# Attention and gated MLP on one core: the scores of the fourth pair of heads from split operands instead of float32 ones

## The chip, the cores and the metric

The kernel runs on one core of one Trainium2 chip. The metric is device microseconds of one execution, lower is better. The kernel before takes 799.14 us in the median of three runs (799.07 to 799.27). The core has five engines that each work through their own instructions in order: PE (matrix products), DVE, ACT and POOL (elementwise work) and SP, which here only issues transfers. Work that depends on another engine's work waits on semaphores; a transfer is waited for in the same way.

## The reference

Eight batches, eight heads, 576 positions, 64 numbers to a head. Attention with a decay, then a gated MLP in which positions are mixed by a matrix:

```python
def _attn_ref(q, k, v, f):
    scores = scale * np.matmul(q, k.transpose(0, 1, 3, 2))
    cum = np.cumsum(np.log(np.clip(f, 0.0001, 1.0)), axis=-1)
    decay = cum[:, :, :, None] - cum[:, :, None, :]
    scores = np.where(causal, -1000000000.0, scores + decay)
    attn = np.exp(scores - np.max(scores, axis=-1, keepdims=True))
    attn = attn / (np.sum(attn, axis=-1, keepdims=True) + 1e-09)
    return np.matmul(attn, v)

def _moe_ref(x, w_in, w_spatial, b_spatial, w_out):
    h = np.maximum(x @ w_in, 0.0)                     # [b, 576, 1024]
    u, v = (h[..., :512], h[..., 512:])
    v_n = (v - mean(v)) / np.sqrt(var(v) + 1e-06)
    v_s = np.einsum('ts,bsd->btd', w_spatial, v_n) + b_spatial[None, :, None]
    return (u * v_s) @ w_out
```

## The kernel before, in words

**Pairs.** The 64 heads are worked on as 32 pairs, P = 0 to 31; four pairs make a batch, so P = 0 to 3 is the whole attention of the first batch. Heads of a pair are h = 0 and 1. Queries and keys of one head lie in one operand of 1216 columns, 640 of queries and 576 of keys, with the 64 dimensions of the head in the partitions. Rows below them carry the decay, so that one product gives score and decay together. The scores of a head (`scores`) are four tiles `sc` of 128 queries by 128, 256, 384 and 512 keys; the last 64 queries of both heads together are two more tiles of 288 keys with one product from each head (`scores_tail`, the "tail"). The first four head tiles are masked and reduced by DVE (L345), exponentiated by ACT (L347) and scaled by POOL (L355) in the buffer `tt` of that head (`tt_67` for h = 0, `tt_68` for h = 1), turned by PE (L401, L414) into `tp`, copied to `ef` (for the first NF = 5 pairs) or split to `eh` and `el`, and multiplied with the values (`attend`, tiles `x`).

**Two ways to make the scores.** Pairs below NQ take their operand as float32: one tile `tf` per head, straight from memory (L288) with two decay rows copied below (L294). One float32 product is two instructions on PE in the trace. From P = NQ on the operand is split in two parts, `hi` and `lo`, whose sum it is: `split(P)` loads the pair's `raw` operand of 128 partitions (L275), ACT rounds it to `hi` (L278) and POOL subtracts to get `lo` in two instructions (L280). `prep(P, h)` then builds two stacked operands per head with six transfers on SP: `ta` holds hi over lo for the queries (L300, L301) and hi again for the keys (L302), `tb` holds hi of the queries (L303), lo of the keys (L304) and four decay rows from `rows_d` (L305). The score is then the sum of two products, one instruction each:

```python
ta = wk.tile([68, QK], F32, name="tf", tag="ta" if P % 2 == 0 else "tb", bufs=2)   # P < NQ
ta = wk.tile([128, QK], F32R, name="ta", tag="ta", bufs=2)                         # P >= NQ
tb = wk.tile([128, QK], F32R, name="tb", tag="tb", bufs=2)
for t in ts:                                                                       # qkt, L260
    mm(o, t[0:r, q0:q0 + 128], t[0:r, k0:k0 + n], first and t is ts[0], final and t is ts[-1])
```

Both ways use the same four buffers: a float32 pair takes two of them (`ta` for even P, `tb` for odd P), a split pair all four. So a split pair's transfers wait for whichever pair had the buffer before.

**Order.** `attention(b)` goes pair by pair: transposes and value products of pair P are written between the scores of pair P + 1. `split(P)` is called in the turn of P - 2, `prep(P, h)` in that of P - 1. `load_first` spreads the loads (L152, L182, L197) and the conversion of the 64-bit weights (`conv64`, L162 to L173, on ACT, DVE and POOL) over the first batch. From then on the MLP of a batch (`moe`) runs between the attention of the next. A scheduler fixes the final order of every engine's instructions when the program is built, from its own estimate of when each can start; on the chip that order doesn't change any more. In the first batch the pool of `sc` tiles has three buffers, and so has that of `tp`.

Of the kernel before, what the change touches and what calls it, by code (L numbers as in the profile page):

```python
# [17 lines left out]

BIG = 1.0e9
NF = 5  # L20
NQ = 4
LEAD = 0.25
S = 576
D = 64
# [14 lines left out]
def attn_gmlp_kernel(ctx: ExitStack, tc: tile.TileContext, qk, v, f, w_in, w_sp, b_sp, w_out, out):  # L39
# [230 lines left out]
    def split(P):  # L270

        if P < NQ:
            return
# [9 lines left out]
    def prep(P, h):  # L283

        p = slice(64 * h, 64 * h + 64)
        if P < NQ:
            ta = wk.tile([68, QK], F32, name="tf", tag="ta" if P % 2 == 0 else "tb", bufs=2)
# [427 lines left out]
```

## Time and profile before

| what | value |
|---|---|
| median of three runs | 799.14 us (799.07 to 799.27) |
| the profiled execution's own time | 797.53 us |
| its span, first to last instruction | 795.7 us |
| mean granted TensorE clock | 0.993 |
| PE busy | 778.9 us, 98% of the span |
| DVE, ACT, POOL busy | 556.6, 534.9, 476.4 us |
| transfers | 103.48 MB, mean 130 GB/s |

In the rows that follow, a row of the timeline gives the start in us from the span's start, the time in us, engine, line, operation, the tiles (out<-in), the shapes and a count; a bracket at its end is the idle time of that engine just before and what ended it. A row of the table by stretch gives for each engine the busy time and the number of instructions in that stretch, then the granted clock of TensorE (1.00 is full speed), the share of time in which the DMA engines were busy, and the rate. PE's instructions overlap: a row's own time is longer than the distance to the next row's start, so what a product costs PE is read from start to start.

### The profile page before, as it was taken

How to read it: one execution, taken by the hardware profiler on the slowest of the kernel's cores; microseconds unless marked ns; L12 is line 12 of the kernel's file. 1: busy time of each engine (PE TensorE's matmuls, PEld its weight loads, DVE VectorE, ACT ScalarE, POOL GpSimd, SP SyncE). 2: the span in 40 equal slices, each digit the busy share in tenths (PEclk: the TensorE clock that was granted, in tenths of full speed). 3: DMA queues.
4: the chain of work that ended last, by engine and by line, in shares of the span. 5: the costliest groups of instructions: out<-in, count | busy, mean ns of one | idle time of the engine just before them, and what ended most of it. 6: DMA issues, size and time to landing. Idle time of an engine off the chain costs nothing.

```text
span 795.7 us, 15502 instructions
## 1 busy us (share of the span) xinstructions
PE 778.9 (98%) x4980; PEld 702.3 (88%) x4981; DVE 556.6 (70%) x1665; ACT 534.9 (67%) x1418; POOL 476.4 (60%) x660
## 2 busy tenths in 40 slices
PE   8999989899999999999999999999999999999997
PEld 4767779798999989998999989999899988998996
DVE  7889778975767667766866668766787658674421
ACT  7787678675777777667766668766686767764431
POOL 5777798664865647465655647554776537643251
PEclk9999999999999999999999999999999999999999
DMA  9967744566454565365454555564555465320001
GB/s 246 239 185 185 188 119 121 119 168 171 103 123 119 153 152 142 102 148 136 104 143 129 133 145 114 131 170 135 141 134 138 108 164 134 78 75 14 28 1 67
DMA packets 41713, 103.48 MB, mean 130 GB/s; under 512 B 6831, under 2 KB 8879, under 8 KB 41568
## 3 DMA queue, kind: packets, MB, share of 16 engines
q1 hardware_dynamic: 41306, 101.96, 49.7%
q8 instruction: 40, 0.66, 0.4%
q10 hardware_dynamic: 326, 0.53, 0.3%
q14 instruction: 41, 0.34, 0.1%
HBM read 39.42 MB, written 10.68 MB: 63 GB/s over the span
## 4 chain that ended last, share of the span: by engine, by line
PE 86%; DVE 6%; ACT 3%; POOL 2%; issue 2%; DMA 1%; ACTq 0%; POOLq 0%; DVEq 0%
PE ps L260 45%; PE sc L260 16%; PE x L260 12%; PE tp L401 8%; PE tp L260 2%; PE tp L414 2%; DVE tt L345 1%; POOL tt L355 1%; DVE el L391 1%; DVE xl L450 1%; DVE wa L163 0%; ACT eh L390 0%; DVE vx L545 0%; ACT tt L347 0%; ACT hi L278 0%
## 5 line engine op out<-in xcount | busy, mean ns | idle before, releaser
L355 POOL TENSOR_SCALAR tt<-tt,sm 128x128 f32<-128x128 f32 (+3 forms) x256 | 142.0, 573 | 74.9 <-DVE sm L351 56.4
L345 DVE CUSTOM_DVE_ANT_0 tt<-sc,zm 128x128 f32<-128x128 f32 (+3 forms) x256 | 122.8, 486 | 85.0 <-PE tp L401 63.4
L390 ACT CAST eh<-tp 128x512 fp32r<-128x512 f32 (+1 forms) x270 | 111.4, 426 | 75.4 <-PE tp L401 50.2
L347 ACT ACTIVATE tt<-tt,nm 128x128 f32<-128x128 f32 (+3 forms) x256 | 144.4, 565 | 23.7 <-DVE nm L345 21.9
L391 DVE TENSOR_TENSOR el<-tp,eh 128x512 fp32r<-128x512 f32 (+1 forms) x270 | 127.2, 485 | 26.2 <-ACT eh L390 23.8
L401 PE MATMUL tp<-ident,tt 128*128 128x128 f32 x640 | 111.6, 277 | 4.1 <-DVE el L391 4.1
L260 PE MATMUL sc<-ta 128*128 128x128 f32 (+1 forms) x336 | 109.1, 330 | 2.5 <-DVE nm L345 2.0
L260 PE MATMUL sc<-tb 68*128 68x128 f32 (+1 forms) x336 | 106.2, 320 | 0.0
L260 PE MATMUL x<-eh,vt 128*128 128x320 f32 (+4 forms) x378 | 102.5, 287 | 0.0
L593 POOL TENSOR_TENSOR gl<-u,gh 128x256 fp32r<-128x256 f32 x64 | 47.7, 745 | 87.7 <-ACT gh L592 78.1
L260 PE MATMUL ps<-xh,win 128*128 128x256 f32 (+1 forms) x464 | 99.3, 304 | 0.4 <-ACT u L570 0.3
L280 POOL TENSOR_TENSOR lo<-raw,hi 128x640 fp32r<-128x640 f32 (+1 forms) x56 | 84.2, 1525 | 16.1 <-ACT hi L278 15.9
L260 PE MATMUL ps<-win,xh 128*128 128x512 f32 x296 | 90.6, 396 | 0.0
L260 PE MATMUL x<-el,vt 128*128 128x256 f32 x324 | 90.1, 303 | 0.0
L401 PEld LDWEIGHTS tp<-ident,tt 128*128 128x128 f32 x640 | 76.3, 141 | 14.2 <-issue 2.7
L449 ACT CAST xh<-x 64x256 fp32r<-64x256 f32 (+1 forms) x128 | 49.8, 394 | 42.3 <-PE x L260 40.3
L260 PEld LDWEIGHTS ps<-xh,win 128*128 128x128 f32 x464 | 76.3, 192 | 2.0 <-ACT u L570 0.9
L260 PE MATMUL ps<-sph,vnh 128*128 128x256 f32 (+1 forms) x240 | 73.2, 305 | 0.4 <-ACT o L618 0.4
L260 PEld LDWEIGHTS x<-eh,vt 128*128 128x128 f32 x378 | 71.3, 190 | 2.5 <-POOL vt L322 0.3
L260 PE MATMUL ps<-wo,gh 128*128 128x512 f32 x224 | 71.9, 405 | 0.0
L260 PEld LDWEIGHTS sc<-ta 128*128 128x128 f32 x336 | 64.3, 191 | 8.6 <-DVE nm L345 4.5
L260 PE MATMUL ps<-sph,vnl 128*128 128x256 f32 (+1 forms) x240 | 71.6, 298 | 0.0
(178 smaller groups left out, 1916.4 us busy)
## 6 DMA issues: line engine op xcount, KB each, us to landing
raw<-in_dram SPq DMA_DIRECT2D x28, 608.0 KB
ta<-hi SPq DMA_DIRECT2D x56, 304.0 KB
vraw<-in_dram SPq DMA_DIRECT2D x32, 320.0 KB
tb<-hi SPq DMA_DIRECT2D x56, 160.0 KB
ta<-lo SPq DMA_DIRECT2D x56, 160.0 KB
out_dram<-o SPq DMA_DIRECT2D x32, 256.0 KB
ta<-hi SPq DMA_DIRECT2D x56, 144.0 KB
tb<-lo SPq DMA_DIRECT2D x56, 144.0 KB
```

The source lines that it names most:

```text
L260: last['mm'] = T.matmul(o, l, r, start=st, stop=sp)
L280: G.tensor_tensor(out=lo[:, c], in0=raw[:, c], in1=f32(hi[:, c]), op=ALU.subtract)
L345: V.tensor_tensor_reduce(out=t, in0=sc[:, 0:n], in1=zm[:, 640 - n:640], scale=-0.125, scalar=3.0e38, op0=ALU.add, op1=ALU.min, accum_out=n ...
L347: last["exp"] = last["exp", P, h, i] = A.activation(t, t, AF.Exp, bias=nm[:, i:i + 1], scale=-1.0, accum_out=se[:, i, 0:1])
L355: G.tensor_scalar(out=t, in0=t, scalar1=sm[:, i:i + 1], scalar2=1.0, op0=ALU.mult, op1=ALU.mult)
L390: A.copy(h_ap, ps)
L391: V.tensor_tensor(out=l_ap, in0=ps, in1=f32(h_ap), op=ALU.subtract)
L401: T.transpose(out=tp[:, (i - c) * 128:(i - c + 1) * 128], in_=tt[h][:, TOFF[i] + 128 * c:TOFF[i] + 128 * c + 128], identity=ident)
L414: T.transpose(out=tp[:, j * 128:(j + 1) * 128], in_=tl[:, c * 128:(c + 1) * 128], identity=ident)
L449: last[P, h] = A.copy(hi, ps[m0:m0 + 64, 0:n])
L450: V.tensor_tensor(out=lo, in0=ps[m0:m0 + 64, 0:n], in1=f32(hi), op=ALU.subtract)
L593: G.tensor_tensor(out=gl[j][:, 0:256], in0=g[:, 0:256], in1=f32(gh[j][:, 0:256]), op=ALU.subtract)
```

## The change

```diff
--- before
+++ after
@@ -18,7 +18,7 @@
 
 BIG = 1.0e9
 NF = 5
-NQ = 4
+NQ = 3
 LEAD = 0.25
 S = 576
 D = 64
```

Pair 3, the fourth and last pair of the first batch, now takes the split way in `split`, `prep` and `qkt`; pairs 0 to 2 stay float32. Its attention weights and values stay float32 (NF is unchanged). Two loads L288 and two copies L294 go; one load L275, one L278, two L280 and twelve transfers L300 to L305 come; 12 float32 products (24 instructions on PE) become 24 products of one instruction.

The scheduler puts much of the first quarter in another order. With buffer numbers left out, PE's first and last rows that differ lie at about 45 and 163 us of the trace; past that, every engine's order is the same as before.

**Pair 3's scores on PE.** Here PE works on the scores of pair 3, head 0 (`sc`), with the transposes of pair 2 (`tp`) and its value products (`x`) between them. Before:

```order
L260 MATMUL sc<-tf 128x256
L260 MATMUL x_601<-ef,vraw 128x192
L260 MATMUL x_601<-ef,vraw 128x64
L401 MATMUL tp<-ident,tt_67 128x128 x2
L260 MATMUL sc<-tf 128x384
L401 MATMUL tp<-ident,tt_67 128x128
L260 MATMUL x_706<-ef,vraw 128x256
L260 MATMUL sc<-tf 128x512
```

The same place with the change:

```order
L260 MATMUL sc<-ta 128x256
L260 MATMUL x_608<-ef,vraw 128x192
L260 MATMUL x_608<-ef,vraw 128x64
L401 MATMUL tp<-ident,tt_67 128x128 x2
L260 MATMUL sc<-ta 128x384
L401 MATMUL tp<-ident,tt_67 128x128
L260 MATMUL sc<-tb 128x128
L260 MATMUL sc<-tb 128x256
L260 MATMUL sc<-tb 128x384
L260 MATMUL x_731<-ef,vraw 128x256
```

The `ta` halves of three tiles stand where the float32 products stood; their `tb` halves come together behind them, and the fourth tile, with the tail, moves behind the first transposes of the next head.

**The transfers for pair 3 on SP.** With the change these rows stand on SP where before there were loads only; a bracket names the semaphores that a row waits on (one of the eight `DMAHW` is that of the transfer eight rows earlier):

```order
L300 DMA ta<-hi 64x1216 [waits DMAHW7_49,PE_49]
L301 DMA ta<-lo 64x640 [waits DMAHW0_49,Pool_49]
L302 DMA ta<-hi 64x576 [waits DMAHW1_49]
L182 DMA w_571<-in_dram 128x4x256 [waits DMAHW2_49]
L182 DMA w_573<-in_dram 128x4x256 [waits DMAHW3_49]
L182 DMA w_575<-in_dram 128x4x256 [waits DMAHW4_49]
L304 DMA tb<-lo 64x576 [waits DMAHW5_49,Pool_49]
L304 DMA tb<-lo 64x576 [waits DMAHW6_49]
```

The last piece of head 0's `tb` (the first of the two L304) is behind three weight loads; L300 waits on PE for the buffer that pair 2's head 0 held.

**Pair 4: the wait of the transfers and the place of the products.** On SP before, the operands of pair 4 were issued in this order (head 0's and head 1's mixed):

```order
L300 DMA ta<-hi 64x1216 [waits DMAHW5_49,Activation_49]
L302 DMA ta<-hi 64x576 [waits DMAHW6_49]
L300 DMA ta<-hi 64x1216 [waits DMAHW7_49]
L303 DMA tb<-hi 64x640 [waits DMAHW0_49,PE_49]
L301 DMA ta<-lo 64x640 [waits DMAHW1_49,Pool_49]
L305 DMA tb<-rows_d 4x1216 [waits DMAHW2_49]
L304 DMA tb<-lo 64x576 [waits DMAHW3_49,Pool_49]
```

With the change:

```order
L305 DMA tb<-rows_d 4x1216 [waits DMAHW6_49,PE_49]
L300 DMA ta<-hi 64x1216 [waits DMAHW7_49,Activation_49]
L302 DMA ta<-hi 64x576 [waits DMAHW0_49]
L303 DMA tb<-hi 64x640 [waits DMAHW1_49]
L301 DMA ta<-lo 64x640 [waits DMAHW2_49,Pool_49]
L300 DMA ta<-hi 64x1216 [waits DMAHW3_49,PE_49]
L304 DMA tb<-lo 64x576 [waits DMAHW4_49,Pool_49]
```

The second L300 fills head 1's `ta`, which pair 3's head 1 now holds until its last score product; before, pair 2 had held it. Head 0's L304 stands right behind that wait.

On PE, the scores of pair 4, head 0, follow the last score product of pair 3, head 1 (the first two rows) like this with the change:

```order
L260 MATMUL sc<-ta 128x512
L260 MATMUL sc<-tb 128x512
L401 MATMUL tp<-ident,tt_67 128x128
L260 MATMUL sc<-ta 128x128
L260 MATMUL sc<-ta 128x256
L401 MATMUL tp<-ident,tt_67 128x128 x2
L260 MATMUL sc<-ta 128x384
L401 MATMUL tp<-ident,tt_67 128x128 x6
L260 MATMUL sc<-tb 128x128
```

Between that last product and the first use of pair 4's `tb` there are nine transposes and three `ta` halves.

## The prediction

> **What bounds the kernel now.** I read the page's busy table first, then the table by stretch around the scores of pair 3, then the chain of waits between 40 and 130 us, since the order changes only there, and last the timeline of PE.
>
> ```profile
> PE 778.9 (98%) x4980; PEld 702.3 (88%) x4981; DVE 556.6 (70%) x1665; ACT 534.9 (67%) x1418; POOL 476.4 (60%) x660
> 40.00:45.00 5.00, 5.00 (x27) 3.56 (x26) 3.60 (x14) 3.94 (x11) 4.29 (x7) 1.00 1.10 356
> 50.00:55.00 5.00, 3.80 (x18) 2.48 (x17) 4.94 (x12) 4.67 (x13) 5.00 (x6) 1.00 0.27 78
> 54.14 1.24 PE L260 MATMUL sc<-tf 66*128 66x288 f32 x4 [1.20 <-DVE nm L345]
> by line: PE x L260 12.8%; PE ps L260 12.6%; PE sc L260 12.3%; POOL tt L355 8.3%; issue 8.2%; PE tp L401 6.6%; DVE tt L345 4.6%; DVE wa L163 4.2%; POOL win L173 2.8%; POOL wa L171 2.8%; POOL vnl L549 2.8%; DVE xl L450 2.1%; DVE spl L205 1.7%
> 81.58 2.14 POOL tt L355 x3
> 83.72 1.27 POOL win L173
> 84.98 1.24 POOL wa L171
> ```
>
> The first row says PE, 98%. Over the whole span that is right: a microsecond of PE work taken away late in the kernel would be a microsecond won. The stretch that the change touches is another matter. At 50 to 55 us PE is busy for 3.80 of 5.00, while DVE (4.94) and POOL (5.00) are full: PE waits 1.20 us for DVE in the middle of pair 3's tail. The chain from 40 to 130 us shows the same: PE's largest lines there are 12.8, 12.6, 12.3 and 6.6%, and from 81.58 us on the chain runs over POOL and DVE pieces, weight conversion among them. So PE time saved at 45 to 60 us is only partly passed on.
>
> **What the scores cost, before and after.** These rows of the timeline are pair 3, head 0, and one half of its tail; below them, the same widths made from split operands in later pairs.
>
> ```profile
> 47.27 0.60 PE L260 MATMUL sc<-tf 66*128 66x256 f32 x2
> 47.71 0.85 PE L260 MATMUL x<-ef,vraw 128*128 128x192 f32 x4
> ...
> 48.77 0.81 PE L260 MATMUL sc<-tf 66*128 66x384 f32 x2
> 49.41 0.27 PE L401 MATMUL tp<-ident,tt 128*128 128x128 f32 x1
> 49.52 0.59 PE L260 MATMUL x<-ef,vraw 128*128 128x256 f32 x2
> 49.96 1.02 PE L260 MATMUL sc<-tf 66*128 66x512 f32 x2
> 50.82 0.49 PE L414 MATMUL tp<-ident,tl 128*128 128x128 f32 x3
> ...
> 51.48 1.24 PE L260 MATMUL sc<-tf 66*128 66x288 f32 x4
> 52.55 0.38 PE L414 MATMUL tp<-ident,tl 128*128 128x128 f32 x2
> ```
>
> ```profile
> 67.30 0.38 PE L260 MATMUL sc<-ta 128*128 128x288 f32 x1
> ...
> 67.94 0.38 PE L414 MATMUL tp<-ident,tl 128*128 128x128 f32 x2
> ...
> 83.02 0.33 PE L260 MATMUL sc<-ta 128*128 128x256 f32 x1
> ...
> 83.31 0.64 PE L260 MATMUL ps<-win,xh 128*128 128x512 f32 x2
> ...
> 85.61 0.42 PE L260 MATMUL sc<-ta 128*128 128x384 f32 x1
> ...
> 86.06 0.40 PE L260 MATMUL sc<-ta 128*128 128x512 f32 x1
> ...
> 86.53 0.49 PE L414 MATMUL tp<-ident,tl 128*128 128x128 f32 x3
> ```
>
> From start to start, float32 takes 0.44 us for 256 keys (47.27 to 47.71), 0.64 for 384, 0.86 for 512 and 1.07 for a tail tile. The two split products take 0.29 (83.02 to 83.31), 0.45, 0.47 and 0.64 (two heads, four products, 67.30 to 67.94). I take the 128-key tile as even. Per head this saves 0.15 + 0.19 + 0.39 = 0.73 us, per tail tile 0.43; twice each makes **-2.3 us of PE work**.
>
> **The work that is added and hidden.** One rounding on ACT and two subtractions on POOL:
>
> ```profile
> 55.29 2.91 POOL L280 TENSOR_TENSOR lo<-raw,hi 128x640 fp32r<-128x640 f32 x2
> 49.19 1.27 POOL L171 TENSOR_TENSOR wa<-w,wa 128x512 f32<-128x512 f32 x1 [4.83 <-DVE sm L350]
> 40.13 0.62 ACT L172 CAST win<-wa 128x512 fp32r<-128x512 f32 x1 [1.13 <-POOL wa L171]
> ```
>
> The 2.91 us on POOL now come at about 37 us, ahead of a wait of 4.83 us for DVE that ends at 49.19; ACT's rounding stands ahead of a wait of 1.13. Both idle times cover them: 0 on the path. Without that cover it would be up to 2.9 us.
>
> What isn't free is DVE. While POOL ran one instruction from 35.98 to 37.25, a DVE instruction that takes 0.41 us elsewhere took 1.41:
>
> ```profile
> 35.98 1.27 POOL L173 TENSOR_TENSOR win<-wa,win 128x512 fp32r<-128x512 f32 x1
> 36.13 1.41 DVE L168 TENSOR_SCALAR wa<-w 128x512 uint32<-128x512 uint32 x1
> ...
> 46.84 0.41 DVE L168 TENSOR_SCALAR wa<-w 128x512 uint32<-128x512 uint32 x1
> ```
>
> Two more POOL instructions can hold up DVE twice by 1.0 us, 2.0 in all; DVE has 1.40 us idle in the stretch from 40 to 45 (5.00 less 3.60). That bounds the cost at 0 to 0.6, if all the idle time serves; I take **+0.3**. [...]
>
> **The wait that goes and the wait that comes.** PE's 1.20 us at 54.14 stand between two products of the tail. With the change the tail comes after the next head's first transposes, so I count that wait as gone: **-1.2** (0 if it only moves). Its place is taken by pair 4. Head 0's last transfer, L304, stands on SP right behind a wait for pair 3's last score product on PE. From that product PE has nine transposes at 0.11 (49.41 to 49.52) and three `ta` halves, some 0.5 by half of the pairs above: 1.5 us of work before it needs that transfer.
>
> ```profile
> 58.23 0.46 SPq L304 DMA_DIRECT2D tb<-lo  x1
> 62.08 0.28 PE L260 MATMUL sc<-tb 68*128 68x128 f32 x1
> ```
>
> From issue to use the same transfer took at most 3.85 us before (58.23 to 62.08; PE didn't wait there, so it may have landed sooner). With one issue of 0.5 ahead of it, it lands up to 4.4 us after the release: a stall of 0 to 2.9 us. I take **+2.4**, near the upper end, since that row is the only one for it. Behind the stalled product stand the value products and all scores of pair 4, and DVE waits for these; behind the blocked L300 on SP stand the rest of pair 4's pieces.
>
> **Pair 3's own last transfer.** L304 follows three weight loads of 512 KB.
>
> ```profile
> 38.29 0.60 PE L401 MATMUL tp<-ident,tt 128*128 128x128 f32 x4
> w<-in_dram SPq DMA_DIRECT2D x12, 512.0 KB
> 54.00:62.00 8.00, 7.86 (x41) 5.89 (x41) 7.03 (x27) 6.61 (x19) 8.00 (x9) 1.00 0.92 209
> ```
>
> `ta` can be issued when pair 2's tail is through, at 38.29 us where the next transposes start; three issues of 0.5 to 0.6 later, at 40, the loads go out. 1.57 MB take 4.4 us at the 356 GB/s of 40 to 45 us, and with 3.85 for the transfer itself it lands at 48.3. PE needs it where the row at 49.52 now stands, less 0.7 for what is no longer ahead of it (0.44 and 0.64, less half of 0.29 and of 0.45): 48.8. I take 0, with 2.6 as the other end, since at the 209 GB/s of 54 to 62 us the loads take 7.5.
>
> **The sum**, against the profiled execution's own 797.53: -2.3 - 1.2 + 2.4 + 0.3 = -0.8, so 796.7. The median of the runs stands 1.6 above that execution; on its scale **798.3**. What 0.8 becomes until 163 us, where both orders are the same again, no row tells: PE waits and gaps of about 2 us at a time lie on that way.
>
> **Rivals.** *The saving goes through, faster.* L304 lands as fast as PE gets there, or POOL's scaling is the later wait in both kernels; then -2.3 - 1.2 = -3.5 is left and 795.6. For it: PE's row at 62.08 didn't wait. Against: DVE is full at 50 to 55 us and gets nothing back.
>
> *The late low parts decide, slower.* One mechanism: L304 comes too late for PE at both pairs. If the loads ahead of it run at 209 GB/s, pair 3 stalls by 2.6; pair 4 by 2.9; and TensorE's clock drops after that.
>
> ```profile
> 108.00:110.00 2.00, 0.88 (x4) 0.48 (x4) 1.90 (x6) 2.00 (x6) 1.10 (x3) 1.00 0.00 0
> 110.00:112.00 2.00, 1.07 (x6) 0.67 (x6) 2.00 (x8) 2.00 (x5) 1.36 (x1) 0.95 0.00 0
> 112.00:114.00 2.00, 2.00 (x10) 2.00 (x9) 2.00 (x5) 2.00 (x6) 2.00 (x2) 0.50 0.00 0
> 114.00:116.00 2.00, 2.00 (x12) 2.00 (x12) 2.00 (x3) 0.63 (x3) 2.00 (x3) 0.69 0.36 71
> ```
>
> PE is busy for 0.88 and 1.07 of two times 2 us, and the granted clock falls right behind that: means of 0.95, 0.50 and 0.69 over 2 us each, so 2 x (0.05 + 0.50 + 0.31) = 1.7 us of full speed are lost. Sum: -2.3 - 1.2 + 2.6 + 2.9 + 1.7 = +3.7, so 802.8. It decides once the stalls and the clock together pass 3.5 + 1.6. Against it: the loads of 40 to 45 us ran at 356. [...]
>
> *The change doesn't do what it says.* If a split product costs PE what a float32 one does, -2.3 falls away: +1.5, 800.6. The rows of both kinds stand against it.
>
> **How the numbers follow.** Forecast 0.42, faster rival 0.28, late low parts 0.25, no saving 0.05. About 0.2% (1.6 us) is what a measurement of this kernel can tell from no change. The forecast's own range is 797.5 to 800.7, all within it. The faster rival and 0.02 from a forecast that gains on its way to 163 us give faster 0.30; the late low parts and 0.03 of the case without a saving give slower 0.28; 0.42 is left for the same. The range, 795.3 to 802.5, takes in the faster rival's 795.6 and most of the way to the slower one's 802.8, which has all three unknown costs (2.6, 2.9 and 1.7) at their far ends; no more than 2 in 10 lie outside.
>
> **What would show it.** Twelve more products `ta` and `tb`, and `tf` down by 24, with the pairs' starts at the distances above. PE's wait at pair 3's tail gone; a wait of PE for a transfer or for POOL at about 60 us, ahead of pair 4's first `tb` product, of 2 to 3 us. No wait of PE at pair 3's first `tb`. POOL's wait ahead of 49 us shorter by about 3. It is wrong if PE waits for pair 3's `tb`, if pair 4's runs on without a wait, or if the places and lengths of the half-clock stretches differ: each of them moves the time by more than my whole sum.

## The result and the profile after

The changed kernel takes 808.69 us (median of four runs, 806.87 to 809.62), the kernel before 799.2 us beside it. The ratio is 1.0115, with a 95% interval from 1.0096 to 1.0133: slower, where I had forecast 798.3 us and no difference that can be told. A second set of four runs of the changed kernel, in a later job, gave 805.8 us (803.56 to 808.16), ratio 1.0087 (1.0061 to 1.0113).

The profiled execution of the changed kernel took 809.62 us, 12.1 us more than the one of the kernel before; its span is 807.8 us. The page's busy row is nearly what it was:

```profile
PE 783.6 (97%) x4981; PEld 707.5 (88%) x4981; DVE 554.8 (69%) x1665; ACT 537.5 (67%) x1419; POOL 479.2 (59%) x662
```

PE is now busy for 783.6 us instead of 778.9, although it has less to do: busy time counts instructions at half clock at their longer time (a `ta` product of 288 columns takes 0.59 us at 56.09, where the clock is halved, and 0.30 at 59.25). So this row can't say where the time is. The timeline of PE can; these are its rows from 45 to 125 us that begin with a wait of 0.44 us or more, and one (70.58) that was expected to:

```profile
52.40 0.64 PE L260 MATMUL sc<-tb 68*128 68x128 f32 x3 [3.54 <-DMA tb<-lo]
...
58.91 0.37 PE L260 MATMUL sc<-ta 128*128 128x288 f32 x1 [1.88 <-DMA ta<-hi]
...
67.46 0.33 PE L401 MATMUL tp<-ident,tt 128*128 128x128 f32 x1 [0.76 <-POOL tt L355]
...
69.22 0.55 PE L401 MATMUL tp<-ident,tt 128*128 128x128 f32 x3 [0.64 <-POOL tt L355]
70.20 0.72 PE L401 MATMUL tp<-ident,tt 128*128 128x128 f32 x3 [0.44 <-POOL tt L355]
70.58 1.10 PE L260 MATMUL sc<-tb 68*128 68x128 f32 x3
...
86.09 2.54 PE L260 MATMUL x<-ef,vraw 128*128 128x320 f32 x10 [1.43 <-DVE xl L450]
...
119.53 0.38 PE L260 MATMUL x<-eh,vt 128*128 128x256 f32 x1 [1.07 <-POOL vt L322]
...
122.24 0.61 PE L260 MATMUL sc<-ta 128*128 128x288 f32 x1 [2.04 <-DVE nm L345]
```

The first two are new: 3.54 us for pair 3's `tb` (head 0), 1.88 us for its `ta` (head 1). The table by stretch shows what stands around them, first before, then after (PE, PEld, DVE, ACT, POOL busy, clock, DMA share, GB/s):

```profile
48.00:52.00 4.00, 4.00 (x20) 2.73 (x19) 3.96 (x10) 3.88 (x10) 2.81 (x3) 1.00 0.28 82
52.00:56.00 4.00, 2.80 (x16) 2.09 (x16) 3.94 (x13) 3.67 (x11) 4.00 (x5) 1.00 0.40 83
```

```profile
48.00:52.00 4.00, 0.86 (x6) 0.51 (x5) 1.91 (x6) 2.06 (x5) 3.30 (x6) 1.00 1.06 230
52.00:56.00 4.00, 3.60 (x16) 3.25 (x17) 2.72 (x9) 2.82 (x8) 1.25 (x2) 0.67 1.03 184
56.00:60.00 4.00, 2.12 (x13) 1.80 (x12) 2.55 (x7) 1.76 (x4) 0.00 (x0) 0.90 0.97 270
60.00:64.00 4.00, 4.00 (x13) 2.68 (x11) 1.55 (x8) 4.00 (x11) 2.90 (x2) 0.57 0.75 173
```

Before, DVE was full in both stretches (3.96 and 3.94 of 4), PE in the first alone. After, no engine is full from 48 to 60 us: the DMA engines are (1.06, 1.03, 0.97). And the granted clock falls to 0.67, 0.90 and 0.57.

**An account of the time.** I took one instruction of PE that stands late enough for both orders to be alike again, the 4000th from PE's last, and split the time to its start in each profiled execution. Idle is the sum of PE's gaps, without the 1.2 us before PE's first instruction, which are the same in both and stand in none of the columns. Clock is half the length of the stretches at half clock, without the gaps in them. Work is the rest.

| kernel | start of that instruction, us | idle | lost to the clock | work |
|---|---|---|---|---|
| before | 182.8 | 8.7 | 4.2 | 168.6 |
| changed | 194.4 | 15.7 | 11.4 | 166.0 |
| difference | +11.6 | +7.0 | +7.2 | -2.6 |

So the saving on PE is there (-2.6, forecast -2.3). Seven microseconds of waits and seven of clock stand against it. From that instruction to the start of PE's last one the two executions take nearly the same (607.6 and 608.0 us). The two profiled executions lie 12.1 us apart and the medians 9.5, so up to 2.6 us of this account belong to these two executions and not to the kernels. The idle part by places: pair 3's transfers +5.4; the wait of 1.20 at its tail gone; pair 4's transposes 1.84 in place of one wait of 0.66; 1.77 for 0.51 from 79 to 90 us; 3.11 for 2.08 where the value products of the second batch begin; 2.29 for 3.24 near the end; +0.2 at the start. The trace has stretches at half clock from 111.8 (3.4 us) and 156.2 (6.8 us) before, and from 53.4, 60.2, 70.4 (3.4 each), 121.6 and 169.4 (6.8 each) after. Each begins during one of the waits or at most 1.3 us behind its end.

**Why the transfers were late.** SP's queue with the change:

```profile
40.09 2.23 SPq L182 DMA_DIRECT2D w<-in_dram  x3
42.42 1.10 SPq L304 DMA_DIRECT2D tb<-lo  x2
43.57 1.42 SPq L275 DMA_DIRECT2D raw<-in_dram  x1
45.09 0.57 SPq L300 DMA_DIRECT2D ta<-hi  x1
```

The loads go out where I put them, from 40.1 us (40 forecast), and L304 right behind them at 42.4. What came of them I read from the semaphore records of the trace. Each of these transfers is sixteen parts; the columns are the start of its issue, the landing of its first and of its last part, and the time from issue to last. The last three rows are the same transfers of pair 3 in a kernel without the three loads ahead of them (run e12 below; `raw` still stands ahead of L300 and L302 there):

```
changed  40.09  L182 w            43.7  44.4   4.3
changed  40.86  L182 w            45.5  49.1   8.3
changed  41.72  L182 w            47.7  51.5   9.8
changed  42.42  L304 tb<-lo, h0   48.4  52.3   9.8
changed  43.57  L275 raw          51.5  55.9  12.3
changed  45.09  L300 ta<-hi, h1   53.0  57.4  12.3
changed  46.40  L302 ta<-hi, h1   54.9  58.8  12.4
e12      40.78  L304 tb<-lo, h0   43.1  43.5   2.7
e12      44.08  L300 ta<-hi, h1   46.9  48.8   4.7
e12      45.23  L302 ta<-hi, h1   48.5  51.5   6.3
```

L304 takes 2.7 us without the three loads ahead of it and 9.8 us behind them. From the second load on, the sixteen parts of a transfer land 3.5 us and more apart, and the two products waited for the last part: it lands at 52.3 and 58.8, and PE's two waits end at 52.40 and 58.91. Everything behind the loads inherits this: `raw` of pair 4, then head 1's `ta`.

### The profile page after: what moved, and what is told of

Its sections match the earlier page's. It is cut to its first block, busy times and chain, and to the rows that moved or that the text cites. A ratio compares the mean times of both kernels' runs of the same rounds, so it can differ in the third digit from the quotient of the medians.

```text
span 807.8 us, 15505 instructions
## 1 busy us (share of the span) xinstructions
PE 783.6 (97%) x4981; PEld 707.5 (88%) x4981; DVE 554.8 (69%) x1665; ACT 537.5 (67%) x1419; POOL 479.2 (59%) x662
## 4 chain that ended last, share of the span: by engine, by line
PE 85%; DVE 6%; ACT 3%; DMA 2%; POOL 2%; issue 2%; SPq 0%; ACTq 0%; POOLq 0%; DVEq 0%
PE ps L260 45%; PE sc L260 16%; PE x L260 12%; PE tp L401 8%; PE tp L260 2%; PE tp L414 2%; DMA ta<-hi 2%; DVE tt L345 1%; POOL tt L355 1%; DVE w L166 1%; DVE el L391 1%; DVE vx L545 1%; DVE xl L450 1%; ACT tt L347 1%; DMA out_dram<-o 0%
## 5 line engine op out<-in xcount | busy, mean ns | idle before, releaser
L355 POOL TENSOR_SCALAR tt<-tt,sm 128x128 f32<-128x128 f32 (+3 forms) x256 | 139.2, 562 | 77.6 <-DVE sm L351 59.9
L260 PE MATMUL sc<-ta 128*128 128x128 f32 (+1 forms) x348 | 113.7, 333 | 7.0 <-DVE nm L345 4.7
L260 PE MATMUL sc<-tb 68*128 68x128 f32 (+1 forms) x348 | 110.6, 324 | 3.5 <-DMA tb<-lo 3.5
L280 POOL TENSOR_TENSOR lo<-raw,hi 128x640 fp32r<-128x640 f32 (+1 forms) x58 | 87.8, 1534 | 21.8 <-ACT hi L278 14.7
L260 PEld LDWEIGHTS sc<-ta 128*128 128x128 f32 x348 | 67.5, 194 | 13.4 <-DVE nm L345 7.5
L260 PEld LDWEIGHTS sc<-tb 68*128 68x128 f32 x348 | 67.8, 196 | 6.3 <-issue 3.8
## 6 DMA issues: line engine op xcount, KB each, us to landing
raw<-in_dram SPq DMA_DIRECT2D x29, 608.0 KB
```

The costliest lines, as they stand in the source:

```text
L260: last['mm'] = T.matmul(o, l, r, start=st, stop=sp)
L280: G.tensor_tensor(out=lo[:, c], in0=raw[:, c], in1=f32(hi[:, c]), op=ALU.subtract)
L355: G.tensor_scalar(out=t, in0=t, scalar1=sm[:, i:i + 1], scalar2=1.0, op0=ALU.mult, op1=ALU.mult)
```

## The experiments

Two theories stood against each other. A: what costs is the place in the queue, behind loads that have not landed. B: the added transfers inside the chip cost by their amount, wherever they stand. The scheduler makes a new order for nearly every edit, so no kernel here differs from the changed one in one instruction's place only. Two pairs come close: e4 has the order of the kernel before on PE, DVE, ACT and POOL, and differs in the queue alone; e2 and e12 have one order on DVE, ACT and POOL and differ on PE in the place of three instructions. Median times are set beside the kernel before in the same job. The account of all runs comes first (profiled execution, us; "to" is the start of the 4000th PE instruction from the last):

| run | median | ratio to before (95%) | to | idle | clock | work |
|---|---|---|---|---|---|---|
| e1 loads one row earlier | 801.25 | 1.0035 (1.0022 to 1.0048) | 188.1 | 13.4 | 7.5 | 165.9 |
| e2 loads one row later | 798.55 | 0.9985 (0.9967 to 1.0002) | 183.5 | 9.8 | 5.0 | 167.6 |
| e3 one float32 pair more | 801.47 | 1.0027 (1.0015 to 1.0039) | 186.6 | 9.8 | 6.3 | 169.2 |
| e4 before, loads as e1 | 798.3 | 0.9994 (0.9983 to 1.0005) | 184.1 | 9.3 | 5.9 | 167.7 |
| e5 loads earliest | 804.14 | 1.0076 (1.0047 to 1.0106) | 188.8 | 13.0 | 7.9 | 166.7 |
| e6 no transfers for pair 3 | 807.53 | 1.0094 (1.0064 to 1.0125) | 187.9 | 13.5 | 6.3 | 166.8 |
| e7 wait filled | 803.6 | 1.0061 (1.0046 to 1.0076) | 187.6 | 11.5 | 5.1 | 169.8 |
| e8 changed again | 805.8 | 1.0087 (1.0061 to 1.0113) | 190.6 | 14.6 | 9.2 | 165.6 |
| e9 before, filled | 800.75 | 1.0026 (1.001 to 1.0042) | 185.9 | 7.1 | 3.4 | 174.2 |
| e10 e2, filled | 801.96 | 1.0047 (1.0032 to 1.0063) | 187.6 | 11.7 | 1.7 | 172.9 |
| e11 loads spread | 807.92 | 1.0109 (1.0094 to 1.0124) | 189.5 | 13.9 | 6.2 | 168.1 |
| e12 loads spread, later | 798.68 | 0.998 (0.9966 to 0.9994) | 183.7 | 9.0 | 6.6 | 166.8 |

The kernel before and the changed one stand in the table above. In e5, e7, e9 and e11 the order still differs from that of the kernel before at that instruction, so their rows compare only roughly. Every kernel with split scores at pair 3 and without extra products has 165.6 to 168.1 us of work, the two of `NQ = 4` without them 167.7 and 168.6. Against the 168.6 of the kernel before, the split is worth 1 to 3 us of PE work in all but one of them (e11); the 0.9 between those two, which have one order, is how far such a figure can be trusted. What decides is idle time and clock: e2 and e12, level with the kernel before, have 14.7 and 15.6 us of both, the others of this kind 19.8 to 27.2.

**e1: the three loads one row of the table earlier.**

```diff
-((2, 0, 0), ((read_sp, 2), (read_sp, 3), (read_sp, 4), (unit, 2))),
-((2, 1, 0), ((read_u, 0), (read_u, 1), (read_u, 2), (unit, 3))),
+((2, 0, 0), ((read_sp, 2), (read_sp, 3), (read_sp, 4), (read_u, 0), (read_u, 1), (read_u, 2), (unit, 2))),
+((2, 1, 0), ((unit, 3),)),
```

> The changed kernel with the three loads L182 of w_in's columns moved ahead of pair 3's transfers (issued behind the loads of w_sp). Theory A (place in the queue: pair 3's last tb piece stood behind 1.57 MB): PE's waits for transfers at about 52 and 59 us (3.5 and 1.9 us) fall below 0.5 together, no half-clock stretch between 50 and 75 us, time 797 to 801. Theory B (amount: twelve more transfers of SBUF to SBUF fill the queue wherever the loads stand): waits of 2 us and more stay, time over 804.

Measured 801.25 us. The wait for `tb` is nearly gone, but others came:

```profile
48.87 0.30 PE L260 MATMUL sc<-ta 128*128 128x128 f32 x1 [1.66 <-DMA ta<-hi]
49.37 0.33 PE L260 MATMUL sc<-tb 68*128 68x128 f32 x1 [0.21 <-DMA tb<-lo]
57.28 0.58 PE L260 MATMUL sc<-ta 128*128 128x288 f32 x1 [4.04 <-DMA ta<-hi]
```

The loads were issued only at 33.7 us, since on SP they stand behind a load that waits for PE, so they were still under way when pair 3's transfers began. SP itself stood for 3.9 us at L302 and for 2.4 at L304 until a load had landed, since each transfer waits for the one eight rows earlier. Theory A had promised waits below 0.5 us in sum, and so missed; but the edit didn't bring the loads out of the way, and it doesn't tell A from B: 5.9 us of waits for transfers are left, 0.5 more than in the changed kernel, though at other places.

**e2: the three loads one row later**, behind pair 3's transfers.

```diff
-((2, 1, 0), ((read_u, 0), (read_u, 1), (read_u, 2), (unit, 3))),
-((3, 0, 0), ((read_u, 3), (read_out, 0), ...
+((2, 1, 0), ((unit, 3),)),
+((3, 0, 0), ((read_u, 0), (read_u, 1), (read_u, 2), (read_u, 3), (read_out, 0), ...
```

> The changed kernel with the same three loads moved behind all of pair 3's transfers. Theory A: as with the loads moved ahead, no wait for transfers at pair 3, 797 to 801; if the weights then come late for their conversion, up to 2 us more at 70 to 110 us. Theory B: over 804.

Measured 798.55 us, level with the kernel before. All of PE's waits from 30 to 150 us:

```profile
52.95 0.40 PE L260 MATMUL sc<-ta 128*128 128x288 f32 x1 [1.04 <-DVE nm L345]
54.51 0.47 PE L260 MATMUL sc<-ta 128*128 128x128 f32 x1 [0.55 <-DVE nm L345]
65.74 0.65 PE L260 MATMUL sc<-ta 128*128 128x128 f32 x3 [2.78 <-DMA ta<-lo]
72.14 0.50 PE L260 MATMUL sc<-ta 128*128 128x288 f32 x2 [0.33 <-DMA ta<-hi]
74.28 0.50 PE L260 MATMUL sc<-tb 68*128 68x288 f32 x2 [1.53 <-DMA tb<-rows_d]
```

Pair 3 waits for no transfer. All twelve are there, so their amount by itself does not make pair 3 late: A, for that place. The loads are now ahead of pair 4's transfers, and it is pair 4 that waits, for 4.6 us in sum. A second thing is to be seen: with pair 3 on time, PE waits for DVE in its tail again, 1.04 and 0.55 us. The wait that I had counted as gone is only covered in the changed kernel, by the wait for `tb` ahead of it.

**e3: pair 4 float32 too** (`NQ = 5`), the step in the other direction.

> The kernel before with pair 4 as float32 too (NQ = 5). Theory A: pair 4's transfers don't hold up PE in the kernel before, so only the products' 2.3 us come on top, in part hidden: 799 to 802. Theory B (each split pair among the first costs several us through its transfers): 791 to 797.

Measured 801.47 us, 2.7 us above the kernel before. That is within what A gave for it and above what B gave. Work is up by 0.6 us, idle by 1.1 and the clock's loss by 2.1. It waits for no transfer. So a kernel with another order of the first 160 us can lose two or three microseconds without any late transfer.

**e4: the kernel before with the loads as in e1**, a control.

> The kernel before (NQ = 4) with the three loads moved ahead as in the first of these runs: the control for that move. Both theories: there is no split operand in the queue at that time, 797.6 to 800.8 (no change). If it is faster by itself, a gain of the first run is the move's and not the split's.

Measured 798.3 us, ratio 0.9994 (0.9983 to 1.0005). PE, DVE, ACT and POOL have the order of the kernel before here, so this is the move in the queue alone: it costs or gains nothing where no split transfers of pair 3 stand beside them.

**e5: the loads at about 20 us**, before all split transfers.

```diff
-((1, 1, 0), ((read_sp, 0), (read_sp, 1), (unit, 1))),
+((1, 1, 0), ((read_u, 0), (read_u, 1), (read_u, 2), (read_sp, 0), (read_sp, 1), (unit, 1))),
```

(and out of the row of pair 2, head 1)

> The changed kernel with the three weight loads put first in the row of the first pair, so that they are issued at about 20 us and have landed long before pair 3's transfers begin. Nothing else is moved by hand. Theory A (the place in the queue, behind loads that have not landed, is what costs): no wait of PE for ta or tb above 0.5 us at pair 3 or pair 4, and with pair 3's float32 work gone 795 to 798.5 us, so at least as fast as the kernel before. Theory B (the transfers inside the chip are slow by themselves, wherever they stand): waits of PE for ta or tb of 2 us or more remain in sum at pairs 3 and 4, and the time is above 800 us.

```profile
52.34 0.40 PE L260 MATMUL sc<-ta 128*128 128x288 f32 x1 [1.04 <-DVE nm L345]
53.91 0.33 PE L260 MATMUL sc<-ta 128*128 128x128 f32 x1 [0.54 <-DVE nm L345]
...
66.69 0.37 PE L260 MATMUL sc<-ta 128*128 128x288 f32 x1 [0.65 <-DMA ta<-hi]
68.41 0.38 PE L260 MATMUL sc<-tb 68*128 68x288 f32 x1 [1.34 <-DMA tb<-lo]
```

Pair 3 waits for no transfer, as A says; L304 landed 3.4 us after its issue. Pair 4 still waits 2.0 us. But 804.14 us is far above what A gave, and above e2. Idle time is 4.3 us more than in the kernel before, of which the transfers make 2.0. Of the rest, 0.3 us lies at 116 to 119 us and 1.2 us from 148 to 165 us, where PE's waits are that much longer than in the kernel before, and in and behind the latter PE ran at half clock for 3.4 us from 151.6 and for 10.2 us from 161.9. So a late operand at pair 3 isn't all: A is right on where pair 3's waits come from and not enough for the time. Taken by the words set down for it, 2 us of waits at pairs 3 and 4 and more than 800 us, this run is as near to B as to A.

**e6: the change on PE alone.** Pair 3's products read two tiles of zeros; there is no split and no transfer for that pair.

```diff
-        if P < NQ:
+        if P <= NQ:
             return
...
+        if P == NQ:
+            if h == 0:
+                for n in ("ta", "tb"):
+                    z = wk.tile([128, QK], F32R, name=n, tag=n, bufs=2)
+                    G.memset(f32(z[:]), 0.0)
+                    zab.append(z)
+            tab[P, h] = tuple(zab)
+            return
```

> The changed kernel without the split and the twelve transfers of pair 3: its split products read two tiles of zeros, so pair 3's true scores are left out. What stays is the change on PE alone. My sum has -2.3 us for it. Theory A and theory B both expect no wait for a transfer at pair 3; the time is 795 to 798.5 us if the saving on PE is passed on, 798.5 to 800 us if it is lost behind DVE and POOL. Above 802 us the transfers would not be the cause of the loss at all.

Measured 807.53 us in the median; the execution with the profile took 802.86, three others 807.5 to 807.6. Neither theory had this, and by the last sentence above the transfers would not be the cause of the loss at all. That is more than the run shows, since this kernel has its own order too; but it does show that an order without any transfer for pair 3 can lose as much as the changed kernel. In the profiled one PE waits at pairs 3 and 4 for DVE, POOL and ACT:

```profile
46.94 1.88 PE L260 MATMUL x<-ef,vraw 128*128 128x320 f32 x6 [0.69 <-DVE xl L459]
53.35 0.40 PE L260 MATMUL sc<-ta 128*128 128x288 f32 x1 [1.31 <-DVE nm L354]
55.75 0.63 PE L410 MATMUL tp<-ident,tt 128*128 128x128 f32 x4 [0.44 <-DVE ef L395]
56.91 0.33 PE L260 MATMUL sc<-ta 128*128 128x128 f32 x1 [0.54 <-DVE nm L354]
63.58 0.33 PE L410 MATMUL tp<-ident,tt 128*128 128x128 f32 x1 [0.44 <-POOL tt L364]
...
73.27 3.09 PE L260 MATMUL x<-ef,vraw 128*128 128x320 f32 x6 [2.18 <-ACT ef L395]
```

These six are 5.6 us where the kernel before had 1.86 (1.20 and 0.66). DVE is as full there as it was:

```profile
48.00:52.00 4.00, 4.00 (x24) 3.09 (x22) 3.90 (x12) 3.83 (x11) 0.94 (x1) 1.00 0.29 75
52.00:56.00 4.00, 2.13 (x14) 1.66 (x13) 3.97 (x9) 3.95 (x11) 4.00 (x6) 1.00 0.03 11
```

So even with nothing of the split left but its products, PE's saved time comes back as waits for the other engines, and more of it than was saved. The 4.7 us that the other three executions took longer go with the clock: their mean granted clock was 0.983, that of the profiled one 0.991, which over some 806 us is 6.4 us less of full speed. Where they lost it, no trace shows.

**e7: the wait filled.** Fourteen products on zeros, of 512 columns, between the third `ta` half and the first `tb` half of pair 3, head 0.

```diff
...
+            fill = ps_a.tile([128, 512], F32, name="x0")
+            for _ in range(14):
+                last["fill"] = T.matmul(fill, zm[:, 0:128], zm[:, 0:512], start=True, stop=True)
+                after(last["fill"], "mm")
...
```

> The changed kernel with 14 extra products on zeros (about 3 us) on PE inside the 3.54 us wait for pair 3's tb; the work and the transfers are the same. Theory of the clock (idle time of PE there halves the clock from 53.4 to 56.8 us and that costs 1.7 us more than the wait): the half-clock stretch behind that wait is gone or shorter, and the time is 1 to 2 us below the changed kernel's in the same job. Rival (the clock's stretches follow something else, such as later waits): the stretch stays or appears elsewhere, and the time is the changed kernel's within 0.7 us or above it.

**e8: the changed kernel again**, beside it.

> The changed kernel itself, beside the others of this job, so that they can be compared with it on one chip: 806.5 to 809.5 us by every theory; a second trace shows whether its waits of 3.5 and 0.4 us at pair 3 and its five half-clock stretches are the same from run to run.

e7 takes 803.6 us (803.45 to 804.25), e8 805.8 (803.56 to 808.16): 2.2 us less in the median, though the runs overlap at one end. With the extra products there is no gap any more at the first `tb`:

```profile
48.92 3.18 PE L349 MATMUL x<-zm 128*128 128x512 bf16 x14
51.75 0.76 PE L260 MATMUL sc<-tb 68*128 68x128 f32 x3
...
56.87 0.38 PE L260 MATMUL sc<-ta 128*128 128x288 f32 x1 [1.97 <-DMA ta<-hi]
```

In e8 the clock is halved from 52.8 for 3.4 us, in e7 not before 57.1, behind the wait of 1.97 us that was left, and the stretch that e8 has at 66.5 is missing too. Work is up by 4.2 us, idle down by 3.1, the clock's loss down by 4.1. Products that compute nothing make the kernel faster here, and what the clock loses is a cost beside the wait itself: idle time and the clock's loss both fell. How much of the 2.2 us is the clock's isn't shown, since e7's order differs from e8's behind that place. e8's waits for transfers are 2.94 and 1.31 us, those of the first trace 3.54 and 1.88: the places are the same, the lengths vary.

**e9 and e10: products on zeros in the waits of other kernels**, to see whether the clock can be won back there. They write into columns of a score tile that its own product leaves free; `FILL` gives their number by pair, head and tile. e9 is the kernel before with `{(6,0,3): 24, (8,0,1): 8, (8,0,3): 30}`, e10 is e2 with `{(3,1,3): 44, (4,0,3): 22, (8,0,1): 8, (8,0,3): 24}`.

```diff
             qkt(sc[:, 0:n], P, h, q0, 0, n, True, True)
+            if n < 512:
+                free = sc[:, n:512]
+            w = 512 - 128 * min(i + 1, 3)
+            for _ in range(FILL.get((P, h, i), 0)):
+                after(T.matmul(free, zm[:, 0:128], zm[:, 0:w], start=True, stop=True), "mm")
```

> The kernel before (NQ = 4) with extra products on zeros on PE, written into unused columns of score tiles: 24 of 128 columns (about 1.4 us) behind the fourth score tile of pair 6, head 0, where PE waits 2.1 us in four pieces from 108 to 111.5 us, 8 of 256 columns (0.9 us) behind the second tile of pair 8, head 0, and 30 of 128 columns (1.7 us) behind its fourth, where PE waits 3.2 us from 153 to 159 us. Theory of the clock (idle time of PE in pieces of 1 to 2 us is what halves the clock): both half-clock stretches of the kernel before (from 111.8 for 3.4 us, from 156.2 for 6.8 us) go or get shorter, and the time falls by 2 to 4 us, to 795 to 797.5 us, though PE has 4 us more to do. Rival (the stretches come from elsewhere, or the waits only move behind the extra products): the time is that of the kernel before within 1 us, or up to 4 us above it.

> The changed kernel with the three weight loads issued one row of the table later (as in the run that was level with the kernel before), and with extra products on zeros in its remaining waits: 44 of 128 columns (2.4 us) behind the last score tile of pair 3, 22 (1.2 us) behind the fourth of pair 4, head 0, 8 of 256 and 24 of 128 columns at pair 8, head 0. Theory of the clock: the half-clock stretches at 54, 75 and 160 us of the kernel with the later loads get fewer, and the time falls from 798.5 to between 794.5 and 797.5 us, faster than both kernels. Rival: within 1 us of 798.5, or above it by what the extra products take.

Both missed: 800.75 and 801.96 us, slower than without the extra products. The loss to the clock did fall, from 4.2 to 3.4 in e9 and from 5.0 to 1.7 in e10. But work rose by 5.7 and 5.3 us. In e9 the scheduler put the first group behind the waits instead of into them, so it added work and covered nothing:

```profile
110.23 0.41 PE L407 MATMUL tp<-ident,tt 128*128 128x128 f32 x2 [0.90 <-DVE el L397]
111.16 0.30 PE L407 MATMUL tp<-ident,tt 128*128 128x128 f32 x1 [0.51 <-DVE el L397]
111.87 2.72 PE L349 MATMUL sc<-zm 128*128 128x128 bf16 x24 [0.41 <-DVE nm L351]
```

In e10 a new wait of 2.80 us for DVE came at 110 us. Less half clock came with the extra products in both; that they gain time in these kernels isn't shown.

**e11 and e12: the loads spread out**, to keep any one of them from standing ahead of a transfer that is needed soon. e11:

```diff
+((2, 0, 0), (..., (read_u, 0), (read_u, 1), (unit, 2))),
+((2, 1, 0), ((unit, 3),)),
+((3, 0, 0), ((read_u, 2), (split_sp, 0), (split_sp, 1), (split_sp, 2))),
+((3, 1, 0), ((read_u, 3), (split_sp, 3), (split_sp, 4), (unit, 4))),
+((4, 0, 0), ((read_out, 0), (unit, 5))),
```

e12 has one load in the first of these rows, `read_u` 1 in that of (3, 0, 0), 2 and 3 in that of (3, 1, 0), and the rest as e11.

> The changed kernel with its five loads spread over the table's rows: two in the row of pair 2, head 0, then one each in the rows of pair 3, head 0, of pair 3, head 1 and (the first L152 load) of pair 4, head 0, so that at most one load stands between a transfer of pair 3 or 4 and its use. Theory of the queue (loads ahead in the queue make the split operands late): PE's waits for ta or tb at pairs 3 and 4 are below 1.5 us in sum, and half-clock stretches before 100 us are at most one. The time then goes by what is left: 797 to 800.5 us if the saved PE work ends up as waits for DVE, ACT and POOL, as in the kernel without transfers; below 797 us if it is passed on. Rival (the transfers are late wherever the loads stand): waits of 3 us or more and above 801 us.

> As the run before, with the loads one step later: one in the row of pair 2, head 0, one in that of pair 3, head 0, two in that of pair 3, head 1, and the first L152 load in that of pair 4, head 0. Two loads then stand ahead of pair 4's low parts. Theory of the queue: no wait above 0.7 us for pair 3's transfers, 1 to 2.5 us for pair 4's ta or tb, and a time within 1.5 us of the run before. Rival (the order on PE alone decides, whatever the queue): waits for transfers like those of the run before, and a time that doesn't go with them.

```profile
69.73 0.37 PE L260 MATMUL sc<-ta 128*128 128x288 f32 x1 [2.81 <-DMA ta<-hi]
```

```profile
51.55 0.40 PE L260 MATMUL sc<-ta 128*128 128x288 f32 x1 [0.50 <-DMA ta<-hi]
52.36 0.40 PE L260 MATMUL sc<-ta 128*128 128x288 f32 x1 [0.28 <-DVE nm L345]
53.92 0.33 PE L260 MATMUL sc<-ta 128*128 128x128 f32 x1 [0.54 <-DVE nm L345]
...
63.96 0.80 PE L260 MATMUL sc<-ta 128*128 128x128 f32 x2 [2.02 <-DMA ta<-lo]
91.94 0.52 PE L414 MATMUL tp<-ident,tl 128*128 128x128 f32 x3 [1.27 <-ACT ef L386]
```

The first fence is e11's longest wait for a transfer, at pair 4; with four more, of 0.22 and 0.39 us at pair 3 and of 0.50 and 0.19 at pair 4, they are 4.1 us in sum where I had expected under 1.5, and 807.92 us: what I had set down for the rival. Ahead of the transfer that this longest wait ends on (L302, issued at 60.64, last part at 69.6) stand one weight load and `raw` of the next pair; it took 8.9 us. Its order differs from that of the kernel before for longer, and 3.4 us of its idle time lie between that 4000th instruction and the 1500th, where the kernel before has 1.0. e12 (second fence) kept to the forecast for the waits, 0.50 at pair 3 and 2.02 at pair 4, but not to the time "within 1.5 us of e11": 798.68 us against 799.66 of the kernel before in the same job, ratio 0.998 (0.9966 to 0.9994). It is the best of the kernels with the change, 1.0 us faster than the kernel before, which is the edge of what can be told; it is 10 us faster than the changed kernel in its first set and 7 us in its second, which ran in other jobs. Against e2, with nearly the same order, 2.1 us less of waits for transfers brought no time (798.68 and 798.55 us).

## Why the prediction was wrong, step by step

- **The step that failed** is "Pair 3's own last transfer", for which I took 0 "with 2.6 as the other end". It measured 3.54 us in the first trace and 2.94 in the second. When PE needs the operand was right: 48.8 forecast, the row ahead of the wait ends at 48.86. When the loads go out was right too (40 forecast, 40.09). What failed is the time of these loads. I gave three loads 4.4 us at the rate of an undisturbed stretch, or 7.5 at a mixed one. The last part of the third landed 11.4 us after the first issue (40.09 to 51.5), with pair 3's transfers, the three loads and `raw` under way together; L304 landed 0.8 us behind it, at 52.3 where I had 48.3. I had also priced one transfer of the pair and not the other: head 1's `ta` stands behind the same loads and behind `raw`, and cost 1.88 us more.
- **The clock** was priced at 1.7 us, and only in the slower rival. It measured 7.2 between the two profiled executions. As in the rows given there, the clock was halved during PE's waits or at most 1.3 us behind their end; the changed kernel has five stretches at half clock up to 180 us, the kernel before two.
- **"-1.2, the wait that goes"** was wrong. In the changed kernel it is gone as forecast, but e2 and e5 have 1.04 us at that place and e6 1.31. It is gone where the 3.54 us for `tb` hold PE up first. The same is true of the -2.3: the work went (-2.6 in the account), but where pair 3's transfers are on time it comes back as idle time or clock: -1.0 of work against +1.0 and +0.8 in e2, -1.8 against +0.2 and +2.4 in e12, -1.8 against +4.8 and +2.1 in e6. I had read DVE at 4.94 of 5.00 and written that saved PE time is "only partly passed on", and then summed it in full.
- **Pair 4's wait** was forecast at 2.4 us and measured 1.84, but in three pieces that POOL's scaling ended. The row at 70.58 shows the first `tb` product without a wait; the late L304 was never the last to come. But it was close: L304 was issued at 67.05 and its last part landed at 70.5, 0.1 us before that product. PE's waits for POOL ran beside the transfer; without them PE would have been there 1.84 us earlier and would have waited for L304 (an estimate from these times). So the length was about right, and another cause ended it.
- **The cover of the added work** held. POOL's subtractions and ACT's rounding ran where I put them, and no wait of PE ends on either. POOL's wait ahead of 49 us is 1.77 us where it was 4.83, shorter by 3.1 as forecast. The +0.3 for DVE behind POOL cost nothing at that place: L169 at 38.04 took 1.42 us beside the subtraction, 0.68 before, but DVE then idled 0.66 us in place of 1.33, and its next instruction (L372) starts at 41.94, before at 42.03:

```profile
37.19 3.53 POOL L280 TENSOR_TENSOR lo<-raw,hi 128x640 fp32r<-128x640 f32 x2
```

```profile
34.81 1.21 ACT L278 CAST hi<-raw 128x1216 fp32r<-128x1216 f32 x1
```

- **What the two products cost** held as well: from start to start 0.32 us for 256 keys (forecast 0.29), 0.44 for 384 (0.45) and 0.54 for a tail tile of both heads, twice the 0.27 from 59.25 to 59.52 (0.64), each at full clock:

```profile
59.25 0.30 PE L260 MATMUL sc<-ta 128*128 128x288 f32 x1
...
59.52 0.30 PE L260 MATMUL sc<-ta 128*128 128x288 f32 x1
...
64.62 0.37 PE L260 MATMUL sc<-ta 128*128 128x256 f32 x1
...
64.94 0.27 PE L401 MATMUL tp<-ident,tt 128*128 128x128 f32 x1
64.97 0.42 PE L260 MATMUL sc<-ta 128*128 128x384 f32 x1
...
65.41 0.82 PE L260 MATMUL x<-ef,vraw 128*128 128x256 f32 x4
```

- **The slower rival** had the right place at pair 3, the right cause (loads ahead in the queue) and the right companion (the clock), and stopped at 802.8 because each of its three ends was too low or misplaced. The test that I named for a wrong forecast, a wait of PE for pair 3's `tb`, is the first row of the profile after.

**What stays open.** That the loads in the queue made pair 3 late is shown; that they are the cause of the whole 9.5 us is not. e2 and e12 show that there are orders in which the change costs nothing; e5 and e6 show that transfers on time for pair 3 are not enough, and every order with the twelve transfers has some 2 us or more of waits for them at pairs 3 and 4 (1.97 in e7, 5.9 in e1). One thing sets e2 and e12 apart from all the other kernels here: PE has no wait from 100 to 130 us, where the others wait for 2.0 to 3.6 us (2.1 in the kernel before, 3.1 in the changed one), most of it for DVE, and where the clock is halved in ten of those twelve. So their level time is a balance of waits gained and lost, and not the mere absence of late transfers. What remains goes with the order of the first 160 us. No run keeps the changed kernel's order and changes only the queue; e4 does that for the kernel before, and e2 against e12 nearly. Why the sixteen parts of a transfer drift apart behind the loads is not shown either.

## What to carry to other kernels

Time a transfer by what is queued ahead of it and still under way, with all that is mixed in there, and follow the same queue to the next operand behind it: one misplaced group of loads made two operands late, by 3.54 and 1.88 us, and not one. Before you credit PE with work that is taken away, look at the engine that is full in that stretch: here it was DVE (3.96 and 3.94 of 4.00 us), and what was saved came back as idle time or clock. A wait that seems to vanish may only be covered by an earlier one, as the one of 1.04 us in e2 and e5 is in the changed kernel. Look for PE's idle time twice, as a wait and in the clock: the changed kernel has 7.0 us more of the one and lost 7.2 us more to the other.

## What the hardware showed that I had not expected

**The clock was halved behind short waits as well as long ones.** These are the stretches at half clock up to 180 us in the profiled executions of the kernel before and of the changed one, with PE's idle time in the 3.4 us ahead of each, the length of the shortest of them:

| kernel | half clock from, us | for, us | idle time ahead, us | the waits in it, us |
|---|---|---|---|---|
| before | 111.8 | 3.4 | 1.87 | 0.94, 0.51, 0.42 |
| before | 156.2 | 6.8 | 1.43 | 1.03, 0.40 |
| changed | 53.4 | 3.4 | 2.44 | the last 2.44 of 3.54 |
| changed | 60.2 | 3.4 | 1.88 | 1.88 |
| changed | 70.4 | 3.4 | 1.51 | the last 0.43 of 0.76, 0.64, 0.44 |
| changed | 121.6 | 6.8 | 2.51 | 1.07, the first 1.44 of 2.04 |
| changed | 169.4 | 6.8 | 1.69 | the last 0.59 of 0.90, the first 1.01 of 1.39; 0.09 in shorter ones |

In two of these seven rows, those of 53.4 and 60.2 us, the idle time is a single long wait; in that of 70.4 us no wait is longer than 0.76 us. Other waits of like length had no half clock behind them: 1.43 us in the changed kernel, up to 86.09 us, and 1.20 us at pair 3's tail in the kernel before, up to 54.14. e3 and e4 have the same 1.20 us there, up to 54.10 in both, and go on differently: the six value products behind it take 3.24 us at half clock in e3 and 1.78 us at full clock in e4:

```profile
54.10 1.24 PE L260 MATMUL sc<-tf 66*128 66x288 f32 x4 [1.20 <-DVE nm L345]
55.17 0.88 PE L401 MATMUL tp<-ident,tt 128*128 128x128 f32 x4
55.84 3.24 PE L260 MATMUL x<-ef,vraw 128*128 128x320 f32 x6
```

```profile
54.10 1.24 PE L260 MATMUL sc<-tf 66*128 66x288 f32 x4 [1.20 <-DVE nm L345]
55.17 0.60 PE L401 MATMUL tp<-ident,tt 128*128 128x128 f32 x4
...
55.83 1.78 PE L260 MATMUL x<-ef,vraw 128*128 128x320 f32 x6
```

What decides between such cases is not shown. The granted clock goes with the time of an execution: in the 31 executions of the kernel before beside e1 to e4 it was 0.992 to 0.995 in the seven below 798 us and 0.990 to 0.991 in the four above 800. A stretch of 3.4 us at half clock counts 1.7 us in the account above if PE is busy in it.

**Transfers behind each other.** A transfer of 64 rows and 576 columns inside the chip took 2.7 us from issue to landing without the three loads ahead of it (e12), 9.8 us in the same queue behind three loads of 512 KB, and 12.4 us with `raw` ahead of it too. The loads suffered as well: four of 512 KB behind each other landed at 41.6, 43.1, 44.6 and 46.0 us in the kernel before, the three of the changed one at 44.4, 49.1 and 51.5. The stretches of 4 us from 40 to 60 us moved 184 to 270 GB/s there, against 356 in the kernel before in the stretch from which I had taken the rate.
